# Four of the sixteen layer-1 tiles by seven half products in four more blocks, fixed staging tiles, and a later check of the softmax sums

## The chip, the cores and the metric

The kernel runs on one core of a Trainium2 chip. The core has TensorE for matrix products (PE in the profile; PEld are its weight loads), VectorE (DVE), ScalarE (ACT), GpSimd (POOL) and SyncE (SP, which here only issues DMAs). Each has its own instruction queue and works through it in order; they meet at semaphores. Matrix products end in PSUM, which has eight banks of 128 x 512 float32. The metric is the time of one execution in microseconds on the device: the median of the runs shown. Beside it stands one execution under the profiler, from which all the rows come.

## The reference

```python
k_all = np.concatenate([beacon_k, k], axis=2)          # 16 + 576 keys
scores = scale * q @ k_all^T, causal on the 576
a = softmax(scores);  x = a @ v_all                    # 8 batches, 8 heads, 64 wide
...
x = x.transpose(0, 2, 1, 3).reshape(8, 576, 512)
h = x.transpose(0, 2, 1) @ U @ V                       # rank 32, over the sequence
u = x + h.transpose(0, 2, 1)
out = u + np.maximum(u @ w_ch1, 0.0) @ w_ch2           # 512 -> 2048 -> 512
```

So: causal attention with 16 extra keys, a low-rank mix over the sequence, and a two-layer network with a residual. Inputs and output are float32; the kernel multiplies in float16 and sums in float32.

## The kernel before, in words

**Two streams on one TensorE.** Attention goes by pairs of heads, p = 0 to 31, four pairs to a batch: scores (L409), exponentials on ACT (L418), the causal mask as a minimum on DVE (`masks_of`, L348), the product with v (L427), and the division by the sum on DVE (L435, L436). The last holds the reciprocals of all softmax sums in `rec`. The network goes by blocks of 512 tokens out of 8 x 576 = 4608, so there are nine blocks, 0 to 8. `mix` and `mix_units` make u of a finished batch and put it, transposed, into the ring `uT` of 2304 columns; block 4 starts at column 2048, so its 512 tokens wrap round (`u_cols` gives two pieces of 256).

**The order is written by hand.** `feed` turns each block whose u is there into a list of units and appends them to `queue`. `fill(n)` takes n units from it; each unit taken also issues one entry of `coming` (loads and other POOL work) and counts down stores. `long_slot` (L1383) lays, for batches 3 to 7, scores, masks, outputs and `fill` calls of one pair in a row: about 30 units to a batch, as many as a block has. So the units of a block lie between the attention of the next batches. What is emitted first comes first in each engine's queue.

**A block.** Layer 1 makes `gT`, sixteen tiles of 128 x 512 of the hidden layer. In blocks 1 to 6 `g_unit` (L628) makes one a unit: four matmuls over the four chunks of the 512 inputs into one bank, then a relu out of it, on DVE in units 2, 5, 11 and 13, on ACT in the others. Layer 2 uses a 2 x 2 scheme with seven products in place of eight: tokens and outputs are halved, `sums` (L617) forms four combinations of `gT` on DVE (from unit 8 on, by the table `SUMS`), `halves_of_w2` once those of the weights, and `c_unit` (L833) issues seven products of two units, 16 matmuls of 256 columns each, into banks named A to F; `after` adds them up on DVE, POOL adds u (`residual`), SP stores.

**Blocks 7 and 8** come after the last attention. There `g_quads` (L649) makes twelve of the sixteen layer-1 tiles by the same scheme with seven products: three sets q = 0, 1, 2 of four tiles, with halves of the inputs and of the tokens. Bank A takes a product, ACT copies it, the next product is added on it in the bank, and so on (`copied`, `half`); bank D does likewise; `summed` adds a copy to F or D on DVE and `relu` follows. `quad_weights` (L580) makes the combined weights on POOL, four sums a set, 12 in all, started at pair 29. Four differences of u (L655) are made by DVE within the block. Their tiles come from the rotating pool `stage` (two buffers to each of two tags), which holds the loaded q and k of the batches before; `kept` is a pool of three float32 tiles. Layer 2 of these blocks is `chain_units`.

**PSUM by a list.** `pst` gives out the eight banks in the order in which they were last emptied, as emitted. A bank that is held over several units is missing from the round.

**The check.** `guard` (L997) compares all sums in `rec` with bounds, nine small instructions on DVE. `guard_sum` adds up over the partitions with one matmul and copies the verdict to `badi`. Every engine then loads it (L1462), and at the end branches into a slower general path if it is not zero. `guard` is emitted after the last attention, `guard_sum` six units before the end of block 7, the load twelve units before the end of block 8.

Of the kernel before, what the change touches and what calls it, by code (L numbers as in the profile page):

```python
# [9 lines left out]
F16 = mybir.dt.float16  # L10
BF16 = mybir.dt.bfloat16
F32 = mybir.dt.float32
# [18 lines left out]
def kernel(  # L31
# [220 lines left out]

    def qk_tiles():

        t = [stage.tile([P, TJ * DM], F16, name=f"st{i}", tag=f"st{i}") for i in range(2)]
# [192 lines left out]
    def mix_units(xb, u0, turned=True):  # L448
# [47 lines left out]
        def end():  # L496
            n = nq[NT - 1]
            ups = pst([P, NCC, n], F32, name="uend")
            for cc in range(NCC) if not turned else ():
                x_into(xb, ups[:, cc, :], cc, [NT - 1], QM, cc == 0)  # L500
            for cc in range(NCC):
                nc.tensor.matmul(
                    ups[:, cc, :], cell["q"], Vend[:, cc, :], start=turned and cc == 0, stop=True,
                    skip_group_check=True,
                )
            settle(1, uT[:, :, ds(u0 % RING + QM, n)], ups)
            emptying(ups)

# [57 lines left out]

    lq = {}

    def quad_tiles():

        t = [stage.tile([P, TJ * DM], F16, name=f"lw{i}", tag=f"st{i}") for i in range(2)]
        w = [[x[:, ds(512 * k, 512)] for k in range(4)] for x in t]
        w.append([pairs.tile([P, 512], F16, name=f"lw{k}", tag=f"pr{k % 2}") for k in range(4)])
        lq["w"] = [[x.rearrange("p (c f) -> p c f", c=2) for x in y] for y in w]
        lq["t"] = [x[:, ds(4 * 512 + 512 * k, 512)].rearrange("p (c x) -> p c x", c=2) for x in t for k in range(2)]
        f = [stage.tile([P, 3, 512], F32, name=f"lk{i}", tag=f"st{i}") for i in range(2)]
        k = [x[:, i, :].rearrange("p (i x) -> p i x", i=2) for x in f for i in range(3)]
        lq["k"] = [(k[2 * q], k[2 * q + 1], k[2 * q]) for q in range(3)]

    def quad_weights(q):  # L580

        def part(c0, d):
            return w1[:, ds(c0, 2), ds(P * d, 2 * P)]

        a11, a12, a21, a22 = part(0, 2 * q), part(2, 2 * q), part(0, HF + 2 * q), part(2, HF + 2 * q)
        s1, s2, s3, s4 = lq["w"][q]
        return [
            lambda o=o, x=x, y=y, op=op: nc.gpsimd.tensor_tensor(out=o, in0=x, in1=y, op=op)
            for o, x, y, op in (
                (s1, a21, a22, ALU.add), (s2, s1, a11, ALU.subtract),  # L590
                (s3, a11, a21, ALU.subtract), (s4, a12, s2, ALU.subtract),
            )
        ]

    def fast_units(t0, dst, last=False, quads=False):


        cell, banks, obs = {}, {}, {}
        cols = u_cols(t0, 512)

# [27 lines left out]
        def g_unit(k):  # L628
            if k == 0:
                begin()  # L630
            dc = order[k]
            g = pst([P, 512], F32, name="gps")
            for cc in range(NCC):
                for at, o, w in cols:
# [3 lines left out]
                    )  # L638
            if k % 2 and cell["turns"]:
                cell["turns"].pop(0)()  # L640
            for x in SUMS.get(k, ()):
                sums(*x)
            if k in (2, 5, 11, 13):
                nc.vector.tensor_scalar_max(out=cell["g"][:, dc, :], in0=g, scalar1=0.0)  # L644
# [4 lines left out]
        def g_quads():  # L649

            at = t0 % RING
            b11, b12, b21, b22 = (uT[:, ds(c, 2), ds(at + x, HT)] for c in (0, 2) for x in (0, HT))
            t1, t2, t3, t4 = lq["t"]
            us = [
                lambda o=o, x=x, y=y: nc.vector.tensor_tensor(out=o, in0=x, in1=y, op=ALU.subtract)  # L655
                for o, x, y in ((t1, b12, b11), (t2, b22, t1), (t3, b22, b12), (t4, b21, t2))
            ]
            held = {}

            def plain(dc):  # L660
                g = pst([P, 512], F32, name="gps")
                for cc in range(NCC):
                    nc.tensor.matmul(  # L663
                        g, w1[:, cc, ts(dc, P)], uT[:, cc, ds(at, 512)], start=cc == 0, stop=cc == NCC - 1
                    )
                nc.scalar.activation(out=cell["g"][:, dc, :], in_=g, func=AF.Relu)
                emptying(g)

# [13 lines left out]
            def of_lw(q, k):  # L682
                return lambda c, i: lq["w"][q][k][:, c, ts(i, P)]

            def copied(q, k):
                nc.scalar.activation(out=lq["k"][q][k], in_=held[q, "A"], func=AF.Copy)  # L686

            def summed(q, bank, k, d, x):
                nc.vector.tensor_tensor(
                    out=cell["g"][:, ds(d, 2), ds(x, HT)], in0=held[q, bank], in1=lq["k"][q][k], op=ALU.add  # L690
                )
# [4 lines left out]
            def step(q, n):  # L696
# [16 lines left out]
                else:  # L713
# [6 lines left out]
                    relu(cell["g"][:, :, HT:512].rearrange("p (h d) t -> p h d t", h=2)[:, :, ds(d, 2), :])  # L720

            slots = [
                (0, 0), (1, 0), (2, 0), (0, 1), (1, 1), (2, 1), (0, 2, 1, 2), (2, 2), 6, 14,
# [5 lines left out]
            def unit(k, slot):  # L729
# [4 lines left out]
                if isinstance(slot, int):  # L734
                    plain(slot)
                else:
# [94 lines left out]
        ]  # L831

        def c_unit(k, j):  # L833
            bank = products[k][0]
            p = pieces(bank)[j]
            product(*products[k], *p)
            for x in sums_at.get(2 * k + j, ()):
                sums(*x)
            if j == 1:
                after(k)  # L840

        def chain_units():

            halves = [(0, 0, HC), (1, 0, HC)]
            small = [(0, 0, HC), (1, 0, P), (1, P, P)] if last else halves

            def grown(k, name, i, c0, w):
                _, a, bm, _ = products[k]
                fresh = (name, i, c0) not in banks
                if fresh:  # L850
                    banks[name, i, c0] = pst([P, w], F32, name="mps" + name)
                ps = banks[name, i, c0]
                for d in range(HF):
                    nc.tensor.matmul(  # L854
                        ps, a()[:, d, ds(P * i, P)], bm[:, d, ds(c0, w)],
                        start=fresh and d == 0, stop=d == HF - 1, skip_group_check=True,
                    )
                return ps

            def first(i, c0, w):  # L860
                ps = grown(0, "A", i, c0, w)
                if i == 0:
                    kept("s1")
                nc.scalar.activation(out=cell["s1"][:, i, :], in_=ps, func=AF.Copy)

# [50 lines left out]
        if quads:  # L916
            return g_quads() + chain_units()
        units = [lambda k=k: g_unit(k) for k in range(NDC)]
        units += [lambda k=k, j=j: c_unit(k, j) for k in range(7) for j in range(len(pieces(products[k][0])))]
# [102 lines left out]
    def load_batch(b):  # L1022
        if b < DT0:
            Ls[b] = qk_tiles()
            emit_loads(b, Ls[b], vss[b % 2])
# [4 lines left out]
    def load_whole(b):  # L1030

        Ls[b] = qk_tiles()
        for i, (src, m) in enumerate(((k[b], nk), (q[b], nq))):
# [128 lines left out]
    FAST = 1  # L1162
    QUADS = (7, 8)
    SUMS = {
# [15 lines left out]
    def fill(n):  # L1180
        while n > 0 and queue:
# [9 lines left out]
            n -= 1  # L1191

    def feed(b):

        while state["t"] < NBLK and 512 * (state["t"] + 1) <= S * (b + 1):
# [7 lines left out]
            else:  # L1203
                units = fast_units(512 * t, dst, t == NBLK - 1, t in QUADS)
            queue.extend(units)
# [41 lines left out]
    with tc.manual_schedule(engines={ENG.PE, ENG.Activation, ENG.DVE, ENG.SP, ENG.Pool}):  # L1247
# [24 lines left out]
        emit_w1(0)  # L1272
        Ls[1] = qk_tiles()
        (kt, qt), _ = Ls[1]
# [187 lines left out]
        n_bad = nc.values_load(badi[0:1, 0:1], min_val=0, max_val=P)  # L1462
# [102 lines left out]
```

## Time and profile before

| | |
|---|---|
| median of 3 runs | 336.14 us (336.02 to 337.72) |
| the profiled execution | 336.39 us, its span 334.5 us |
| clock granted to TensorE | 1.00 |
| PE busy | 326.3 us, 98% of the span |
| DVE, ACT, POOL busy | 251.7, 190.8, 148.5 us |
| blocks 3, 4, 5, 6 start (layer 1) | 146.0, 180.6, 215.3, 249.9 us |
| blocks 7 and 8 start | 279.3, 304.4 us |
| last matmul ends about | 329.4 us |

Times in the profile count from the start of the span. A row of a group gives the line of the kernel, the engine, the operation with output and input tiles, the count, then the busy time, the mean of one in ns, and how long the engine stood idle ahead of them and for what. A row of a timeline gives start, length, engine, line and count; in square brackets is the idle time before it and who ended it. Matmul durations include the way through the array; the distance of starts tells the rate. The same holds in part for DVE, where the next instruction can start a little before the row of the last one ends.

### The profile page before, as it was taken

To read this page: it belongs to the slowest core of one execution; us is meant where nothing else is said; L and a number is where in the kernel's file an instruction comes from. 1 tells how busy PE (TensorE), PEld (TensorE's weight loads), DVE (VectorE), ACT (ScalarE), POOL (GpSimd) and SP (SyncE) were. 2 spreads that over 40 slices of the span, in tenths; PEclk is the share of its full clock that TensorE was granted. 3 is DMA by queue.
4 is the path that set the end of the run, shared out by engine and by line. 5 is a ranking of instruction groups with operands and counts; after the bars stand their busy time and mean duration, and the time that the engine had idled before them with its cause. 6 is when DMAs were issued, how large, how long until landed. Compare 5 with 4: busy or idle time off the path is not lost.

```text
span 334.5 us, 9085 instructions
## 1 busy us (share of the span) xinstructions
PE 326.3 (98%) x3614; PEld 223.9 (67%) x3614; DVE 251.7 (75%) x572; ACT 190.8 (57%) x413; POOL 148.5 (44%) x185
## 2 busy tenths in 40 slices
PE   8899999999999999999999999999999999999993
PEld 3565555555577656865588888754875588788793
DVE  6675888678897668765777677667777978797692
ACT  5967961788972677257734684469435403703700
POOL 8987824766236540677066904150398014010010
PEclk9999999999999999999999999999999999999999
DMA  8999999999999993999999996955213513206113
GB/s 164 144 176 161 158 201 196 199 184 151 81 150 150 135 181 74 130 200 171 151 124 174 144 132 110 117 130 120 51 42 94 91 47 110 49 32 127 31 36 101
DMA packets 150561, 41.99 MB, mean 126 GB/s; under 512 B 131312, under 2 KB 149936, under 8 KB 150512
## 3 DMA queue, kind: packets, MB, share of 16 engines
q0 software_dynamic: 87568, 18.18, 73.3%
q1 hardware_dynamic: 62144, 22.41, 36.5%
q10 hardware_dynamic: 800, 0.75, 0.7%
q8 instruction: 30, 0.49, 0.6%
q14 instruction: 19, 0.16, 0.2%
HBM read 37.45 MB, written 9.44 MB: 140 GB/s over the span
## 4 chain that ended last, share of the span: by engine, by line
PE 91%; ACT 5%; DVE 1%; issue 0%
PE gps L635 24%; PE po L427 8%; PE mpsD L760 6%; PE sps L409 6%; PE mpsF L760 4%; PE cps L965 4%; PE mpsA L854 4%; PE gps L939 4%; PE mpsE L760 3%; PE qpsA L674 3%; PE mpsC L760 3%; PE mpsA L760 3%; PE mpsB L760 3%; ACT expt L376 2%; PE mpsD L854 2%; PE gps L663 2%
## 5 line engine op out<-in xcount | busy, mean ns | idle before, releaser
L418 ACT ACTIVATE expt<-sps 128x496 f16<-128x496 f32 (+2 forms) x192 | 82.2, 547 | 41.6 <-PE sps L409 41.6
L635 PE MATMUL gps<-uT,w 128*128 128x512 f16 (+1 forms) x448 | 91.9, 349 | 0.2 <-ACT kT L1091 0.2
L780 POOL TENSOR_TENSOR ob<-ob,ut 128x512 f32<-128x512 f32 x26 | 31.3, 1207 | 131.2 <-DVE ob L780 121.5
L760 PEld LDWEIGHTS <-gT 128*128 128x128 f16 x704 | 66.4, 98 | 10.4 <-issue 2.6
L635 PEld LDWEIGHTS <-w 128*128 128x128 f16 x448 | 40.4, 98 | 32.0 <-issue 2.5
L646 ACT ACTIVATE gT<-gps 128x512 f16<-128x512 f32 x72 | 42.9, 619 | 25.2 <-PE gps L635 19.9
L624 DVE TENSOR_TENSOR gT<-gT 128x1024 f16<-128x1024 f16 (+3 forms) x90 | 47.5, 550 | 1.0
L240 POOL DMA_DIRECT2D vs<-in_v_dram x50 | 39.9, 812 | 14.1 <-DMA w<-in_moe_w_ch_dram 11.1
L427 PEld LDWEIGHTS <-expt 128*128 128x128 f16 x900 | 33.8, 98 | 9.8 <-issue 1.5
L427 PE MATMUL po<-vs,expt 128*128 128x65 f16 x900 | 36.4, 194 | 0.3
L348 DVE TENSOR_TENSOR expt<-expt,bigmask 128x768 f16<-128x768 f16 x54 | 34.4, 676 | 1.4 <-ACT expt L418 1.2
L436 DVE TENSOR_TENSOR xb<-po,rec 128x320 f16<-128x320 f32 x64 | 31.5, 492 | 2.2
L435 DVE RECIPROCAL rec<-po 128x5 f32<-128x5 f32 x64 | 12.1, 189 | 19.5 <-PE po L427 19.1
L644 DVE TENSOR_SCALAR gT<-gps 128x512 f16<-128x512 f32 x24 | 16.6, 690 | 13.1 <-PE gps L635 12.6
L686 ACT ACTIVATE lk<-qpsA 128x512 f32<-128x512 f32 x18 | 10.3, 597 | 25.6 <-PE qpsA L674 14.8
L409 PE MATMUL sps<-qT,kT 64*128 64x80 f16 (+4 forms) x288 | 22.6, 281 | 0.0
L376 ACT ACTIVATE expt<-sps 128x496 f16<-128x496 f32 (+2 forms) x48 | 20.4, 569 | 0.7 <-PE sps L370 0.7
L854 PEld LDWEIGHTS <-gT 128*128 128x128 f16 x208 | 19.0, 98 | 2.4
L1038 POOL DMA_DIRECT2D st<-in_q_dram x20 | 16.9, 866 | 6.9 <-DVE ob L780 6.5
L409 PEld LDWEIGHTS <-kT 64*128 64x128 f16 x288 | 10.3, 94 | 12.8 <-issue 8.2
L1038 POOL DMA_DIRECT2D st<-in_k_dram x20 | 16.9, 859 | 1.5 <-DMA st<-in_q_dram 1.5
L939 PE MATMUL gps<-uT,w 128*128 128x512 f16 x64 | 16.2, 380 | 0.1
(151 smaller groups left out, 479.3 us busy)
## 6 DMA issues: line engine op xcount, KB each, us to landing
out_dram<-ob SPq DMA_DIRECT2D x33, 256.0 KB, 3.6
vs<-in_v_dram POOLq DMA_DIRECT2D x18, 128.0 KB, 6.9
w<-in_moe_w_ch_dram POOLq DMA_DIRECT2D x4, 512.0 KB, 6.4
w<-in_moe_w_ch_dram POOLq DMA_DIRECT2D x2, 1024.0 KB, 12.8
st<-in_k_dram POOLq DMA_DIRECT2D x12, 128.0 KB, 6.3
st<-in_q_dram POOLq DMA_DIRECT2D x12, 128.0 KB, 7.0
st<-in_k_dram POOLq DMA_DIRECT2D x4, 288.0 KB, 11.8
st<-in_q_dram POOLq DMA_DIRECT2D x4, 288.0 KB, 12.9
```

What stands on the lines that cost most here:

```text
L240: nc.gpsimd.dma_start(out=dst[a : a + nq[j], j, :, :], in_=src[hs, ds(q0[j], nq[j]), :].rearrange("h p d -> p h d"))
L348: nc.vector.tensor_tensor(out=e, in0=e, in1=bigmask[:, :, :].rearrange("p (a b) x -> p a b x", b=2), op=ALU.min)
L409: nc.tensor.matmul(banks[i][:, ds(at0 + o, w)], kT(hp, c, ch), qT[hp, c, ds(qa, w)], start=True, stop=True, skip_group_check=len(unit) > 1,)
L418: nc.scalar.activation(out=at[p][3][i][:, ds(AT[g], gw[g])], in_=bank[:, ds(at0, gw[g])], func=AF.Exp, scale=scale)
L427: nc.tensor.matmul(po[:, j, :], ex[0 : nk[c], ds(blk[(c, j)], P)], vs[0 : nk[c], ds(c * H * E + h * E, E)], start=(c == 0), stop=(c == j),)
L436: nc.vector.tensor_tensor(out=xb[:, :, ds(h * D, D)], in0=po[:, :, 0:D], in1=r.broadcast_to([P, NT, D]), op=ALU.mult)
L624: nc.vector.tensor_tensor(out=o[:, ds(d0, n)], in0=x[:, ds(d0, n)], in1=y[:, ds(d0, n)], op=op)
L635: nc.tensor.matmul(g[:, ds(o, w)], w1[:, cc, ts(dc, P)], uT[:, cc, ds(at, w)], start=(cc == 0 and o == 0), stop=(cc == NCC - 1), skip_grou ...
L646: nc.scalar.activation(out=cell["g"][:, dc, :], in_=g, func=AF.Relu)
L760: nc.tensor.matmul(ps, a()[:, d, ds(P * i, P)], bm[:, d, ds(c0, w)], start=fresh and d == 0 and i == 0, stop=d == HF - 1, skip_group_check ...
L854: nc.tensor.matmul(ps, a()[:, d, ds(P * i, P)], bm[:, d, ds(c0, w)], start=fresh and d == 0, stop=d == HF - 1, skip_group_check=True,)
L1038: coming.append(lambda d=dst, s=src, a=m[j] - nq[j], n=m[j], j=j: nc.gpsimd.dma_start(out=d[a:n, j, :, :], in_=s[:, ds(q0[j], nq[j]), :].r ...
```

## The change

Blocks 3 to 6 get `PARTS` 1: in layer 1 set 0 (tiles 0, 1, 8, 9) is made by `g_quads`' seven half products, in four units of 8, 8, 4 and 8 matmuls of 256 columns; the other twelve tiles stay plain, three of their relus on DVE. The number of units, 16 and 14, is as before. The sums of `gT` start in unit 11 instead of 8. The differences of u for the next block (`u_sums`) are made on DVE in units 10 to 13 of the layer 2 before. In layer 2 of these blocks the second product is added onto the first one's bank, after ACT has copied that, and ACT copies the result out; before, it had a bank of its own and a DVE addition. Blocks 7 and 8 have the three sets as before; set 0's copies lie in `kept` tiles and its weights in the `pairs` tiles, made from pair 15 on.

The pool `stage` gives way to four tiles that are allotted once; batch b loads into tiles 2 (b mod 2) and the next one, and the differences of u have the last sixth of each, which the whole-batch loads of batches 4 to 7 leave free.

`guard` moves from the end of the attention to after unit 4 of block 8, `guard_sum` to after the second unit of block 8's layer 2, the load of the verdict from twelve to eight units before the end.

```diff
-    stage = ctx.enter_context(tc.tile_pool(name="stage", bufs=2))
...
+    staged = [const.tile([P, TJ * DM], F16, name=f"st{i}", tag=f"st{i}") for i in range(4)]
...
+        t = staged[2 * (b % 2) : 2 * (b % 2) + 2]
...
+    def quad_tiles(q):
+
+        if q == 0:
+            w = [pairs.tile([P, 512], F16, name=f"lw{k}", tag=f"pr{k % 2}") for k in range(4)]
+        else:
+            w = [staged[q - 1][:, ds(512 * k, 512)] for k in range(4)]
+            f = staged[q + 1][:, 0 : 2048].bitcast(F32).rearrange("p (k i x) -> p k i x", k=2, i=2)
+            lq["k", q] = (f[:, 0], f[:, 1], f[:, 0])
+        lq["w", q] = [x.rearrange("p (c f) -> p c f", c=2) for x in w]
...
+    def u_sums(t0, eng):
+
+        b11, b12, b21, b22 = (u_half(t0, c, x) for c in (0, 2) for x in (0, HT))
+        t1, t2, t3, t4 = (staged[i][:, 5 * DM : 6 * DM].rearrange("p (c x) -> p c x", c=2) for i in range(4))
...
+        return [lambda a=a: one(*a) for a in ((t1, b12, b11), (t2, b22, t1), (t3, b22, b12), (t4, b21, t2))]
...
+            def plain(k, dc):
+                layer_one(dc, not quads and k in (2, 11, 13))
...
+            def space(q, k):
+                if k < 2:
+                    cell["k", q, k] = lq["k", q][k] if q else kept("k")
+                else:
+                    cell["k", q, k] = cell["k", q, 0]
+                return cell["k", q, k]
...
+            if not quads:
+                slots = [2, (0, 0), 10, (0, 1), 3, 11, (0, 2), 4, (0, 3), 12, 5, 13, 6, 14, 7, 15]
+                late = {11: ((0, 0, 4),), 12: ((1, 0, 4),), 13: ((2, 0, 4),), 14: ((0, 4, 3),), 15: ((1, 4, 3),)}
...
+        if parts:
+            sums_at = {0: ((2, 4, 3),), 1: ((0, 7, 1), (1, 7, 1)), 2: ((2, 7, 1), (3, 0, 4)), 3: ((3, 4, 4),)}
...
+        def first(i, c0, w):
+            ps = grown(0, "A", i, c0, w)
+            if i == 0:
+                kept("s1")
+            nc.scalar.activation(out=cell["s1"][:, i, :], in_=ps, func=AF.Copy)
+
+        def second_on(i, c0, w):
+
+            ps = grown(1, "A", i, c0, w)
+            if i == 0:
+                out_tile("11")
+            nc.scalar.activation(out=obs["11"][:, i, :], in_=ps, func=AF.Copy)
+            freed(("A", i, c0))
+            if i:
+                residual("11", 0, 0)
...
-    QUADS = (7, 8)
+    PARTS = {3: 1, 4: 1, 5: 1, 6: 1, 7: 3, 8: 3}
+    AHEAD = 10
...
+            if p == P6 + 3:
+                quad_tiles(0)
+                coming.extend(quad_weights(0))
             if p == NP - 3:
-                quad_tiles()
-                coming.extend([u for q in range(3) for u in quad_weights(q)])
+                for n in (1, 2):
+                    quad_tiles(n)
+                    coming.extend(quad_weights(n))
...
-        guard()
-
-
-        queue.insert(len(queue) - 37, guard_sum)
-        fill(len(queue) - 12)
+        queue.insert(len(queue) - 26, guard)
+
+        queue.insert(len(queue) - 14, guard_sum)
+        fill(len(queue) - 8)
```

More of the change, by code (lines that the diff above doesn't have):

```diff
@@ L630, in g_unit, with between, layer_one @@
                 begin()
-            dc = order[k]
+            def between():
+                if k % 2 and cell["turns"]:
+                    cell["turns"].pop(0)()
+                for x in SUMS.get(k, ()):
+                    sums(*x)
+            layer_one(order[k], k in (2, 5, 11, 13), between)
+        def layer_one(dc, on_vector, between=lambda: None):
             g = pst([P, 512], F32, name="gps")
@@ L638, in g_unit @@
                     )
[L639 to L643, printed above, removed]
+            between()
+            if on_vector:
                 nc.vector.tensor_scalar_max(out=cell["g"][:, dc, :], in0=g, scalar1=0.0)
@@ L720, in step, with unit @@
                     relu(cell["g"][:, :, HT:512].rearrange("p (h d) t -> p h d t", h=2)[:, :, ds(d, 2), :])
+            if not quads:
+                slots = [2, (0, 0), 10, (0, 1), 3, 11, (0, 2), 4, (0, 3), 12, 5, 13, 6, 14, 7, 15]
+                late = {11: ((0, 0, 4),), 12: ((1, 0, 4),), 13: ((2, 0, 4),), 14: ((0, 4, 3),), 15: ((1, 4, 3),)}
+                def unit(k, slot):
+                    if k == 0:
+                        begin()
+                    plain(k, slot) if isinstance(slot, int) else step(*slot)
+                    if k % 2 and cell["turns"]:
+                        cell["turns"].pop(0)()
+                    for x in late.get(k, ()):
+                        sums(*x)
+                return [lambda k=k, slot=slot: unit(k, slot) for k, slot in enumerate(slots)]
             slots = [
@@ L845, in chain_units @@
             small = [(0, 0, HC), (1, 0, P), (1, P, P)] if last else halves
[L847 to L864, printed above, removed]
             def second(i, c0, w):
```

93 lines of the change are left out of this document (52 added, 41 removed).

## The prediction

> **What bounds the kernel now.** I read the page first, then the waits of TensorE (PE), the table of windows cut at block borders, the chain that ended last, the groups by shape, and the timelines of single blocks.
>
> ```profile
> span 334.5 us, 9085 instructions
> PE 326.3 (98%) x3614; PEld 223.9 (67%) x3614; DVE 251.7 (75%) x572; ACT 190.8 (57%) x413; POOL 148.5 (44%) x185
> ```
> ```profile
> PE gps L635 <- ACT kT L1091: 0.2, 1, 0.2
> ```
> ```profile
> 146.00:165.24 19.24, 19.24 (x206) 10.27 (x205) 13.14 (x27) 14.28 (x30) 11.09 (x14) 1.00 2.12 180
> 165.24:180.58 15.34, 15.34 (x170) 12.56 (x169) 11.64 (x25) 6.47 (x16) 7.35 (x8) 1.00 1.31 139
> ...
> 304.40:317.06 12.66, 12.66 (x103) 9.81 (x101) 9.69 (x21) 8.63 (x15) 0.00 (x0) 1.00 0.45 76
> 317.06:334.50 17.44, 12.27 (x128) 11.02 (x126) 11.28 (x25) 1.36 (x3) 1.16 (x1) 0.99 0.21 66
> ```
>
> The window columns are length, then busy time (and instructions) of PE, its weight loads, DVE, ACT and POOL, then PE's granted clock. The first two windows are layer 1 and layer 2 of block 3, the last two block 8 with the tail. PE is busy for all of each but the last, at full clock, and from block 1 on its list of waits has the one row of 0.2 us. A busy PE could still hide a slow rate, so I took the rate from the chain (start, length, pieces):
>
> ```profile
> 150.03 4.42 PE gps L635 x20
> ...
> 163.04 1.73 PE gps L635 x8
> ...
> 197.76 1.75 PE gps L635 x16
> ...
> 284.63 1.31 PE qpsA L674 x12
> ```
>
> A 512-column matmul takes 1.73/8 = 0.216 us, a 256-column one 1.31/12 = 0.109 us, in block 7's half products too: time goes by columns. What takes columns away here shortens the run, if nothing new makes PE wait.
>
> **The change: TensorE.** In blocks 3 to 6 four of the sixteen layer-1 tiles (16 matmuls of 512 columns, 16 x 0.216 = 3.46 us) become seven half products of four matmuls of 256 (28 x 0.109 = 3.06 us): 0.40 us less. Block 4 wraps round the ring, so its plain tiles already are 32 matmuls of 256 columns (32 x 1.75/16 = 3.50 us): 0.44 less. Sum: 3 x 0.40 + 0.44 = **1.65 us** (unrounded). Layer 2 keeps its seven products; that the second lands on the first one's bank changes no column. Blocks 7 and 8 keep their matmuls.
>
> The Trainium skill, "TensorE: Matmul & The Clock Gate", section Back-to-back issue gap, speaks against this: it gives about 131 ns sustained for 512 columns and 81 ns for 128. My estimate between them for 256 is 98 ns, so 28 x 98 = 2.74 us against 16 x 131 = 2.10 us, 0.65 us slower a block, 336.1 + 4 x 0.65 = 338.7 in all. The rows above do not show that; the section's isolated gap (518 and 262 cycles) agrees with them.
>
> **Work beside it.**
>
> ```profile
> L646 ACT ACTIVATE gT<-gps 128x512 f16<-128x512 f32 x72 | 42.9, 619 | 25.2 <-PE gps L635 19.9 <-issue 4.3 <-ACT ob L980 0.7
> L624 DVE TENSOR_TENSOR gT<-gT 128x1024 f16<-128x1024 f16 x38 | 27.0, 727 | 0.0
> L644 DVE TENSOR_SCALAR gT<-gps 128x512 f16<-128x512 f32 x24 | 16.6, 690 | 13.1 <-PE gps L635 12.6
> L686 ACT ACTIVATE lk<-qpsA 128x512 f32<-128x512 f32 x18 | 10.3, 597 | 25.6 <-PE qpsA L674 14.8 <-DVE ob L780 10.7
> L689 DVE TENSOR_TENSOR gT<-qpsD,lk 128x512 f16<-128x512 f32 x12 | 7.9, 685 | 4.1 <-ACT lk L686 2.2 <-PE qpsD L674 1.9
> L674 PEld LDWEIGHTS <-lw 128*128 128x128 f16 x96 | 9.3, 98 | 1.3 <-issue 0.2
> L588 POOL TENSOR_TENSOR lw<-w 128x512 f16<-128x512 f16 x6 | 7.2, 1208 | 0.0
> L780 DVE TENSOR_TENSOR ob<-mpsF,kept 128x512 f32<-128x512 f32 x8 | 5.5, 691 | 4.4 <-PE mpsF L760 4.4
> L797 ACT ACTIVATE kept<-mpsA 128x512 f32<-128x512 f32 x6 | 3.6, 597 | 8.6 <-PE mpsA L760 8.6
> L694 DVE TENSOR_SCALAR gT<-gT 128x1024 f16<-128x1024 f16 x6 | 2.6, 427 | 0.2
> L694 DVE TENSOR_SCALAR gT<-gT 128x512 f16<-128x512 f16 x6 | 1.8, 294 | 0.2
> L864 ACT ACTIVATE kept<-mpsA 128x256 f32<-128x256 f32 x4 | 1.5, 384 | 1.5 <-PE mpsA L854 1.5
> ```
> ```profile
> L655 DVE TENSOR_TENSOR lw<-uT,lw x4: 418/422/1261, 280.4 to 308.7; 128x512 f16<-128x512 f16 x4
> ```
>
> DVE in layer 1 gets three sums out of PSUM (3 x 0.685), two relus (0.427 + 0.294), loses one relu (0.690) and passes one of the gT sums (0.727) on to layer 2: +1.36, so 14.5 of 18.8 us. In layer 2 it gets that sum and four sums of u for the next block (4 x 0.42) and loses the add of product F (0.691): +1.72, so 13.4 of 15.3. ACT swaps three relus (0.619) for three copies and a relu (4 x 0.597, the relu at the copies' price), +0.53; in layer 2 four half copies (0.384) replace one (0.597), +0.94. Neither engine fills its window, so these cost nothing unless one comes late. The four POOL sums of weights for set 0 are not new: they move forward from the run-up to block 7 to batch 3's last head pair. That is 4 x 1.21 = 4.8 us of POOL's queue, one sum to a unit; a load queued after them slips by those 4.8 us at most. First use is in unit 3 of block 3, over twenty units later, so I put it at nothing; without that cover it would be 4.8 us, once.
>
> A sum of u took 0.42 us, but once 1.26, when a POOL add ran beside it. The Trainium skill, "GPSIMD Engine Reference", section Specifications, says GpSimd shares SBUF interfaces with VectorE when an instruction reads two SBUF inputs; the trace agrees, 1.26 against 0.42. So a sum of u costs 0.42 to 1.26; I take 0.42, the median.
>
> **Hand-offs that can make PE wait.** Block 3, start of layer 1:
>
> ```profile
> 144.36 0.69 DVE L780 TENSOR_TENSOR ob<-mpsE,kept 128x512 f32<-128x512 f32 x1 [1.86 <-PE mpsE L760]
> 144.97 1.98 DVE L348 TENSOR_TENSOR expt<-expt,bigmask 128x768 f16<-128x768 f16 x2
> ...
> 148.68 0.19 DVE L435 RECIPROCAL rec<-po 128x5 f32<-128x5 f32 x1 [0.50 <-PE po L427]
> 148.91 0.49 DVE L436 TENSOR_TENSOR xb<-po,rec 128x320 f16<-128x320 f32 x1
> ```
> ```profile
> 149.86 2.01 ACT L418 ACTIVATE expt<-sps 128x496 f16<-128x496 f32 x4 [1.05 <-PE sps L409]
> 151.73 1.12 ACT L646 ACTIVATE gT<-gps 128x512 f16<-128x512 f32 x2
> ```
>
> Of the four sums of u two fall into DVE's 1.86 us of idle time before 144.36, two behind the masks, so DVE falls 0.8 us behind. Step 0 of the set then puts a sum and a relu (0.98 us) ahead of the second division of an attention output, where 0.5 us of idle time takes part of it: that division ends at about 150.7 instead of 149.4. It frees a bank. With A and D held, two banks fewer go round, and I count the next user of this one as layer 1's unit 4, at 150.03 + 0.88 = 150.9: 0.2 us of cover. ACT: the copy of step 1 starts at 151.73, behind four exponentials, and ends at 152.33; A's next half starts at 150.03 + 3 x 0.884 = 152.7. Its copy, behind two relus, ends at about 154.0, and step 3 starts at about 154.4 (today's five tiles end at 154.45; less 0.44, and one attention output between); the sum from D ends 0.7 later, 0.2 before D's second half. So the margins are 0.2 to 0.4 us, in each of four blocks. I take 0: below nothing is excluded, since PE waits for none of these now; above, a missed hand-off costs its lateness, at most the 0.41 of a block in the rival below.
>
> Layer 2, where product B needs the last of its gT sums:
>
> ```profile
> 159.67 0.69 DVE L644 TENSOR_SCALAR gT<-gps 128x512 f16<-128x512 f32 x1 [1.46 <-PE gps L635]
> 160.28 1.02 DVE L348 TENSOR_TENSOR expt<-expt,bigmask 128x768 f16<-128x768 f16 x2
> ...
> 165.91 1.28 DVE L624 TENSOR_TENSOR gT<-gT 128x768 f16<-128x768 f16 x4
> ```
> ```profile
> 169.56 0.55 PE mpsB L760 x5
> ```
>
> Today those sums end at 165.91 + 1.28 = 167.2 and B starts at 169.6. In the new order they begin with unit 11, whose relu starts at about 159.3 (0.41 earlier). Laid end to end from there: two relus 1.4, masks 1.0, three large sums 2.2, two at most as large 1.5, two divisions 1.4, and the four pieces of the last row 1.3, in all 8.8, so 168.1 at the latest. B then starts at 169.2: at least 1 us of cover.
>
> **The check of the sums and the fixed tiles.**
>
> ```profile
> 261.30 0.33 DVE L999 MEMSET good<- 128x320 f16 x1
> ...
> 263.87 0.16 DVE L1007 TENSOR_SCALAR bad<-allg 128x1 f16<-128x1 f32 x1
> ```
> ```profile
> 308.73 0.42 DVE L655 TENSOR_TENSOR lw<-uT,lw 128x512 f16<-128x512 f16 x1
> 310.78 1.89 DVE L689 TENSOR_TENSOR gT<-qpsD,lk 128x512 f16<-128x512 f32 x3 [1.63 <-ACT lk L686]
> 313.62 0.69 DVE L689 TENSOR_TENSOR gT<-qpsD,lk 128x512 f16<-128x512 f32 x1 [0.96 <-PE qpsD L674]
> ```
> ```profile
> L1462 PEldq TENSOR_LOAD <-badi x1: 487/487/487, 318.4 to 318.4; - x1
> ```
>
> The check is 2.7 us of DVE (261.3 to 264.0), in layer 1 of block 6, where it also was late work. It now follows unit 4 of block 8, right behind 308.73. There DVE idles 1.63 and then 0.96 us, so the three sums from D slip by about 1.1 us and the next by 0.2. PE needs the first of the three at 313.0 and gets it at about 312.6. The load of the verdict moves by four units, behind a sum that is done by then. Cost 0; without that idle time up to 1.1 us, once; a gain of one load (0.49) is possible. The fixed tiles hold the same batches in the same memory; only what a load waits for can change, and PE's waits show no load after the start: 0.
>
> **Sum.** 1.65 us against the profiled execution: 336.39 (span 334.5 and 1.9 around it) to 334.74, on the median 336.14 - 1.65 = **334.5**, 0.49% faster. About 0.5% (334.46) is what a measurement can tell from no change, so the forecast sits on that line.
>
> **Rivals.** *Given back at hand-offs*: for it, margins of 0.2 to 0.4 us; against, each holds on paper. With 0.41 us of waits in each block nothing is left: 336.1. *More than the columns*: the verdict's load drops from the tail, 334.5 - 0.5 = 334.0; against it, PE loses nothing visible there now. *Slower, sums late for product B*: all four sums of u at 1.26 (+3.4 us of DVE) and no idle time to recover in; decides from 1 us of lag at unit 11, then B waits 2.4 us in each block: 334.5 + 4 x 2.4 = 344.1. Against it, the 4.3 us that DVE idles in layer 1. *Slower, small matmuls pay for their weights*: the load's 98 ns comes on top of the 109 ns, 28 x 0.207 = 5.8 against 3.46 us, +2.3 in four blocks: 345.5. The row of 12 in 1.31 us stands against that. The Trainium skill's sustained figures, above, are a milder case of it. *The change does not do what it says*, PE follows the exponentials of ACT and the columns become idle time: 336.1 again, counted with the first; ACT's 14.28 of 19.24 us speaks against.
>
> **Chances.** Forecast 0.70, half of it beyond 0.5%; more 0.03; given back 0.20; sums late 0.05; weights 0.02. Faster 0.35 + 0.03 = 0.38, same 0.35 + 0.20 = 0.55, slower 0.07. Range: 333.9 (with the gain of a load) to 336.2 (all given back).
>
> **What would show it.** Right: layer 1 of blocks 3, 5, 6 shorter by 0.4 us, PE busy throughout, no wait at the new lines, layer 2 as before. Wrong: gaps of PE at the second or third half on A, a plain tile late behind the fourth division, a gap ahead of B, a stall in block 8 behind the check, or half products above 0.44 us per four.

## The result, and the profile after

| | before | after |
|---|---|---|
| median, nine runs each | 335.6 us (335.31 to 337.72) | 334.03 us (333.70 to 334.53) |
| ratio after / before | | 0.9944 [0.9927, 0.9962] |
| the profiled execution, its span | 336.39, 334.5 us | 334.53, 332.9 us |
| body: first plain tile of block 3 to the end of the last product | 183.50 us | 182.28 us |

The changed kernel is faster, by 1.57 us between the medians. The ratio goes by the means (335.97 and 334.10 us), in which before's longest run of 337.72 weighs more. The forecast was 1.65 us and 334.5 us. The page of after:

```profile
span 332.9 us, 9194 instructions
PE 324.4 (97%) x3646; PEld 226.9 (68%) x3646; DVE 264.9 (80%) x600; ACT 195.8 (59%) x429; POOL 149.3 (45%) x185
```

PE is busy 1.9 us less, with 32 matmuls more, and DVE 13 us more. The list of PE's waits has, from block 1 on, a row that before's has not:

```profile
PE sps L410 <- DVE ob L820: 0.2, 1, 0.2
```

The windows of after, with the columns as in the prediction (layer 1 and layer 2 of block 3):

```profile
146.51:165.35 18.84, 18.84 (x218) 11.42 (x217) 14.36 (x32) 14.70 (x31) 11.08 (x14) 1.00 2.10 148
165.35:180.69 15.34, 15.34 (x170) 12.54 (x169) 13.38 (x28) 7.23 (x19) 7.46 (x8) 1.00 1.35 142
```

Layer 1 of block 3 is 18.84 us long against 19.24, layer 2 is 15.34 as before, and PE is busy throughout. DVE has 14.36 us in layer 1 (14.5 forecast) and 13.38 in layer 2 (13.4 forecast).

The start of block 3 lies up to 1.7 us apart in the profiles of the kernels here (145.5 to 147.2), so I compare lengths. The body begins with the first plain tile of block 3, in PE's timeline, and ends with the last product, in the chain that ended last. Before, in these two views:

```profile
145.84 1.03 PE L635 MATMUL gps<-uT,w 128*128 128x512 f16 x4
```
```profile
327.56 1.78 PE mpsD L854 x24
```

After:

```profile
146.34 1.03 PE L664 MATMUL gps<-uT,w 128*128 128x512 f16 x4
```
```profile
326.84 1.78 PE mpsD L880 x24
```

Before: 327.56 + 1.78 - 145.84 = 183.50. After: 326.84 + 1.78 - 146.34 = 182.28, so 1.22 less. By blocks, from first tile to first tile, blocks 3, 4 and 5 took 34.58, 34.74 and 34.58 us before and 34.19, 34.30 and 34.18 after: 0.39, 0.44 and 0.40 less, the forecast's columns within a hundredth. Block 6 has as many columns fewer and did not get shorter. PE there, before (first plain tile, third scores of the batch, the tile behind them, first half product of block 7):

```profile
249.74 1.03 PE L635 MATMUL gps<-uT,w 128*128 128x512 f16 x4
...
253.34 0.39 PE L409 MATMUL sps<-qT,kT 64*128 64x336 f16 x6
253.66 2.55 PE L635 MATMUL gps<-uT,w 128*128 128x512 f16 x11
...
279.11 0.60 PE L674 MATMUL qpsA<-uT,w 128*128 128x256 f16 x4
```

and after:

```profile
249.01 1.03 PE L664 MATMUL gps<-uT,w 128*128 128x512 f16 x4
...
252.62 0.31 PE L410 MATMUL sps<-qT,kT 64*128 64x336 f16 x1
253.10 0.37 PE L410 MATMUL sps<-qT,kT 64*128 64x336 f16 x5 [0.17 <-DVE ob L820]
253.41 0.61 PE L690 MATMUL qpsA<-st,lw 128*128 128x256 f16 x4
...
278.46 0.60 PE L690 MATMUL qpsA<-uT,w 128*128 128x256 f16 x4
```

The block took 279.11 - 249.74 = 29.37 us before and 278.46 - 249.01 = 29.45 after. The scores take 253.41 - 252.62 = 0.79 us from start to next start instead of 0.32. The list of waits says 0.2 us, since one matmul of the group had run and its modelled end covers part of the gap; the distance of starts gives the whole of it, 0.47 us. That is block 6's 0.40 of columns and a little more. The releaser is DVE's last addition of the layer 2 before, which empties the bank that these scores go to. DVE in after, up to that addition:

```profile
245.62 1.03 DVE L593 TENSOR_TENSOR st<-uT 128x512 f16<-128x512 f16 x1
246.69 1.26 DVE L593 TENSOR_TENSOR st<-uT,st 128x512 f16<-128x512 f16 x1
247.87 0.68 DVE L820 TENSOR_TENSOR ob<-mpsE,kept 128x512 f32<-128x512 f32 x1
248.47 2.34 DVE L349 TENSOR_TENSOR expt<-expt,bigmask 128x768 f16<-128x768 f16 x2
250.73 1.38 DVE L593 TENSOR_TENSOR st<-uT 128x512 f16<-128x512 f16 x1
252.04 0.41 DVE L593 TENSOR_TENSOR st<-uT,st 128x512 f16<-128x512 f16 x1
252.37 0.68 DVE L820 TENSOR_TENSOR ob<-mpsD,kept 128x512 f32<-128x512 f32 x1
```

and POOL beside it, making the weight sums of sets 1 and 2:

```profile
246.33 1.34 POOL L605 TENSOR_TENSOR st<-w 128x512 f16<-128x512 f16 x1
...
248.93 1.47 POOL L605 TENSOR_TENSOR st<-w,st 128x512 f16<-128x512 f16 x1
250.36 1.47 POOL L820 TENSOR_TENSOR ob<-ob,ut 128x512 f32<-128x512 f32 x1
```

Three of the four sums of u take 1.03, 1.26 and 1.38 us, the fourth, with POOL idle from 251.83, takes 0.41. The addition ends at 252.37 + 0.68 = 253.05, and PE goes on at 253.10.

### The profile page after: what moved, and what is told of

It is laid out like the page before. It is cut to its first block, busy times and chain, and to the rows that moved or that the text cites. A ratio compares the mean times of both kernels' runs of the same rounds, so it can differ in the third digit from the quotient of the medians.

```text
span 332.9 us, 9194 instructions
## 1 busy us (share of the span) xinstructions
PE 324.4 (97%) x3646; PEld 226.9 (68%) x3646; DVE 264.9 (80%) x600; ACT 195.8 (59%) x429; POOL 149.3 (45%) x185
## 4 chain that ended last, share of the span: by engine, by line
PE 86%; DVE 6%; ACT 5%; DMA 1%; issue 1%; DVEq 0%
PE gps L664 21%; PE mpsA L880 8%; PE po L428 8%; PE sps L410 6%; PE mpsD L800 5%; PE qpsA L690 5%; PE cps L1019 4%; PE gps L993 4%; PE mpsB L800 3%; PE mpsE L800 3%; PE mpsC L800 3%; PE qpsD L690 3%; PE mpsF L800 2%; PE mpsD L880 2%; ACT expt L377 2%; ACT w L377 2%
## 5 line engine op out<-in xcount | busy, mean ns | idle before, releaser
L664 PE MATMUL gps<-uT,w 128*128 128x512 f16 (+1 forms) x400 | 84.9, 354 | 0.2 <-ACT kT L1145 0.2
L664 PEld LDWEIGHTS <-w 128*128 128x128 f16 x400 | 36.6, 98 | 29.0 <-issue 1.8
L672 ACT ACTIVATE gT<-gps 128x512 f16<-128x512 f32 x68 | 40.6, 618 | 19.6 <-PE gps L664 14.1
L709 ACT ACTIVATE kept<-qpsA 128x512 f32<-128x512 f32 x18 | 10.8, 602 | 22.6 <-PE qpsA L690 12.0
L670 DVE TENSOR_SCALAR gT<-gps 128x512 f16<-128x512 f32 x20 | 13.8, 689 | 11.4 <-PE gps L664 11.3
L880 PE MATMUL mpsA<-w,gT 128*128 128x256 f16 x160 | 19.0, 273 | 0.0
```

The costliest lines, as they stand in the source:

```text
L664: nc.tensor.matmul(g[:, ds(o, w)], w1[:, cc, ts(dc, P)], uT[:, cc, ds(at, w)], start=(cc == 0 and o == 0), stop=(cc == NCC - 1), skip_grou ...
L880: nc.tensor.matmul(ps, a()[:, d, ds(P * i, P)], bm[:, d, ds(c0, w)], start=fresh and d == 0, stop=d == HF - 1, skip_group_check=True,)
```

## The experiments

My theory after the result: the gain is the columns of blocks 3 to 6, and block 6 loses its share in that one wait, because DVE works through the sums of u beside POOL's weight sums. The rivals: fixed tiles, early weights or the later check bring part of the gain; the wait at 253 is not what block 6 lost; the two additions onto one bank in layer 2 matter.

**e1_no_parts** keeps all of the change but the half products of blocks 3 to 6.

```diff
-    PARTS = {3: 1, 4: 1, 5: 1, 6: 1, 7: 3, 8: 3}
+    PARTS = {7: 3, 8: 3}
```

> The changed kernel with blocks 3 to 6 made the old way (all sixteen layer-1 tiles plain, old layer 2, no sums of u ahead); the fixed tiles, the early weights of set 0 and the late check stay. Theory (the gain is TensorE's columns): the time from block 3's first matmul to the last one is 183.3 us as before (it was 182.1 in the changed kernel), and the whole is as before within 0.2 us. Rival (the gain lies in the tail, behind the late check: from the last matmul to the end of the span 4.3 us after against 5.2 before): the span still gains some 0.9 us, and the whole is 0.9 us faster than before.

Measured: 335.33 us, ratio to before 0.9995 [0.9981, 1.0009]. The body's ends, in PE's timeline and in the chain:

```profile
145.87 1.03 PE L664 MATMUL gps<-uT,w 128*128 128x512 f16 x4
```
```profile
327.59 1.78 PE mpsD L880 x24
```

183.50 us, as before. Without the half products nothing is left of the body's gain. Of the time, the interval leaves room for 0.6 us faster to 0.3 us slower than before (the medians lie 0.28 us apart).

**e2_check_moved** is the kernel before with the check alone moved.

```diff
-        guard()
-        queue.insert(len(queue) - 37, guard_sum)
-        fill(len(queue) - 12)
+        queue.insert(len(queue) - 26, guard)
+        queue.insert(len(queue) - 14, guard_sum)
+        fill(len(queue) - 8)
```

> The kernel before with nothing changed but the place of the check, of its sum and of the verdict's load. Theory: no change within 0.2 us, the tail behind the last matmul stays near 5.2 us and moves only by what it scatters by itself. Rival (the later load shortens the tail): 0.5 to 0.9 us faster than before, tail near 4.3 us. A third: block 8 pays for the check on DVE, up to 1.1 us slower, with a gap on PE behind it.

Measured: 335.84 us, 1.0007 [0.9999, 1.0016]. The time gains nothing from the later load. The profile warns of something else: its body is 183.97 us, 0.47 more than before's. 0.25 of that is in block 5, which the edit doesn't touch: PE takes 0.78 us for eight scores there instead of 0.52, at full clock, and the trace names no engine that it waits for. A block's length in a single profile can be off by that much.

**e3_no_block6** leaves block 6 as it was.

```diff
-    PARTS = {3: 1, 4: 1, 5: 1, 6: 1, 7: 3, 8: 3}
+    PARTS = {3: 1, 4: 1, 5: 1, 7: 3, 8: 3}
```

> The changed kernel with half products in blocks 3, 4 and 5 only; block 6 the old way, and so no sums of u in block 5's layer 2. Theory (block 6 gave its 0.40 us back in one wait for a bank, 0.47 us at its third scores): the same time as the changed kernel within 0.1 us, block 3's first to the last matmul about 182.1 us, and no wait of PE at 253. Rival (each block brings 0.4 us and the wait was chance): 0.4 us slower than the changed kernel, 182.5 us.

Measured: 334.17 us, 0.9958 [0.9944, 0.9971], body 182.31 against after's 182.28 (block 5 has 0.11 more than after's here, and block 6, with 29.38, 0.07 less). PE in block 6:

```profile
252.06 0.39 PE L410 MATMUL sps<-qT,kT 64*128 64x336 f16 x6
252.38 3.84 PE L664 MATMUL gps<-uT,w 128*128 128x512 f16 x17
```

The third scores take 0.32 us again, with 0.40 us more of columns behind them. So block 6's half products gain 0.40 and lose it.

**e4_weights_early** starts the weight sums of sets 1 and 2 two head pairs earlier.

```diff
-            if p == NP - 3:
+            if p == NP - 5:
                 for n in (1, 2):
```

> The changed kernel with the POOL sums of the weights of sets 1 and 2 started two head pairs earlier, so that they are done before DVE makes the sums of u for block 6. Theory (those sums of u took 1.03, 1.26 and 1.38 us instead of 0.41 since POOL's sums ran beside them, and that made DVE late with the bank): sums of u at 0.41 to 0.5 us, no wait of PE at 253, block 3's first to the last matmul 181.7 us, 0.4 us less than the changed kernel. Rival (DVE is late from its own amount of work): the wait stays, 182.1 us. Against both: the POOL sums now stretch masks and sums of gT in block 5's layer 1 and PE waits there.

Measured: 336.41 us, 1.0017 [1.0006, 1.0028]. The wait at block 6 went: the sums of u took 0.41, 1.26, 0.41 and 0.41 us there, and the block 28.98 us, 0.39 less than before. But POOL's sums now lay in layer 1 of block 5, beside the masks and the sums of `gT`, and block 5 took 36.67 us instead of 34.18. PE's waits and one row of DVE:

```profile
PE sps L410 <- DVE xb L437: 1.2, 1, 1.2
...
PE gps L664 <- DVE xb L437: 0.5, 1, 0.5
```
```profile
229.36 2.94 DVE L349 TENSOR_TENSOR expt<-expt,bigmask 128x768 f16<-128x768 f16 x2
```

Two masks take 2.94 us where they took 1.02. The same POOL work two pairs earlier costs more than block 6 had lost. So POOL beside DVE, and not DVE's own amount of work, made the wait.

**e5_weights_split** makes set 1's weights where after does and set 2's two pairs later.

```diff
-            if p == NP - 3:
-                for n in (1, 2):
-                    quad_tiles(n)
-                    coming.extend(quad_weights(n))
+            if p in (NP - 3, NP - 1):
+                n = 1 if p == NP - 3 else 2
+                quad_tiles(n)
+                coming.extend(quad_weights(n))
```

> The changed kernel with the POOL sums of set 2's weights made two head pairs later (beside block 6's layer 1), those of set 1 where they were, so that POOL is free while DVE makes the sums of u for block 6. Theory (POOL's sums beside them made DVE late with the bank that PE's third scores of block 6 need): those sums take 0.41 us but for one beside a residual addition, no wait of PE in block 6, block 3's first to the last matmul 181.7 us against 182.1, the whole 0.4 us faster than the changed kernel. Rival (contention only moves: the later POOL sums stretch DVE work in block 6's layer 1 as they did in block 5's when they came earlier): 182.1 us or more, with a wait of PE between 255 and 268.

Measured: 334.44 us, 0.9967 [0.9955, 0.9978], body 182.62. PE's waits, and DVE in block 6:

```profile
PE qpsD L690 <- DVE gT L712: 0.7, 1, 0.7
```
```profile
251.84 1.23 DVE L717 TENSOR_SCALAR gT<-gT 128x512 f16<-128x512 f16 x1
...
254.22 2.89 DVE L349 TENSOR_TENSOR expt<-expt,bigmask 128x768 f16<-128x768 f16 x2
```

The third scores took 0.32 us again, with sums of u of 0.41, 1.26, 0.41 and 0.41. The wait had moved: POOL's sums of set 2 ran from 251.78 to 256.7, the relu of 0.29 us took 1.23, the masks 2.89, and the sum from D came 0.7 us late for D's second half.

**e6_sums_twice** makes each sum of u of blocks 3 to 6 twice over.

```diff
-            return us[n - AHEAD : n - AHEAD + 1] if n >= AHEAD else []
+            return us[n - AHEAD : n - AHEAD + 1] * 2 if n >= AHEAD else []
```

> The changed kernel with every sum of u for blocks 3 to 6 made twice in a row: DVE gets 1.7 us more ahead of each of these blocks, up to 2.5 where POOL runs beside it. Theory (in blocks 3 to 5 DVE's last addition of layer 2 frees its bank 1.5 us ahead of the scores that need it, in block 6 not at all): 0 to 1 us of waits in each of blocks 3 to 5, 1 to 2.5 more in block 6, in all 1.5 to 5 us slower than the changed kernel. Rival (the 0.2 to 0.4 us of cover that the prediction counted at the second division's bank): at least 1 us in every block, 4 us and more in all.

Measured: 338.82 us, 1.0093 [1.0077, 1.011], body 187.10, 4.8 more than after. The largest wait, in block 6:

```profile
253.58 0.62 PE L428 MATMUL po<-vs,expt 128*128 128x65 f16 x15 [1.62 <-DVE expt L349]
```

Blocks 3 and 4 took 1.35 and 1.31 us more than after's (PE waited at the third scores and at a plain tile), block 5 took no more, and block 6 took 2.17 more. The total fits the theory and the rival alike. By blocks neither holds: the theory allowed blocks 3 and 4 at most 1 us each, and the rival asked at least 1 us of block 5. The eight sums there took 0.42 to 0.44 us each and two masks 1.02, with POOL's last instruction ended at 212.6; in blocks 3 and 4, with POOL additions beside them, two of the eight took 1.71 us together and the masks 1.98. So DVE has cover for eight sums where POOL rests, and not where it adds.

**e7_old_layer2** takes layer 2 of blocks 3 to 6 from the kernel before.

```diff
-            if parts and k < 2:
-                (first, second_on)[k](*p)
-            else:
-                product(*products[k], *p)
+            product(*products[k], *p)
...
-            if j == 1 and not (parts and k < 2):
+            if j == 1:
```

> The changed kernel with layer 2 of blocks 3 to 6 as before: product F in a bank of its own, added to the first by DVE. Theory (layer 2 brings no time, it only spares DVE an addition of 0.69 us and a bank): the same as the changed kernel within 0.2 us, 182.1 us from block 3's first to the last matmul, or slightly more in block 6. Rival (the accumulation is needed, since DVE is the late engine in layer 2): 0.3 to 0.7 us more in each of four blocks, 1.2 to 2.8 us slower.

Measured: 334.08 us, 0.9951 [0.9937, 0.9964]: by time the same as after. The trace shows more. Its body is 181.88 us, 0.40 less than after's, and all of that is block 6 (29.06 us). The third scores there, and the first sum of u:

```profile
253.52 0.46 PE L410 MATMUL sps<-qT,kT 64*128 64x336 f16 x6
253.92 0.61 PE L690 MATMUL qpsA<-st,lw 128*128 128x256 f16 x4
```
```profile
246.49 0.68 DVE L593 TENSOR_TENSOR st<-uT 128x512 f16<-128x512 f16 x1
```

The scores take 0.40 us, so 0.08 of the wait is left. In after POOL's queue is released by ACT's copy of the second product, 9.5 us before block 6; here by DVE's addition, 9.9 us before it:

```profile
239.53 1.15 POOL L820 TENSOR_TENSOR ob<-ob,ut 128x512 f32<-128x512 f32 x1 [15.23 <-ACT ob L897]
```
```profile
240.03 1.16 POOL L820 TENSOR_TENSOR ob<-ob,ut 128x512 f32<-128x512 f32 x1 [15.33 <-DVE ob L820]
```

So the weight sums run 0.4 us earlier, and the first sum of u takes 0.68 instead of 1.03 us. The addition on one bank saves DVE an addition, and by this one trace it costs block 6, through POOL, what it lost.

**e8_steps_together** puts the four steps of set 0 next to each other instead of between plain tiles.

```diff
-slots = [2, (0, 0), 10, (0, 1), 3, 11, (0, 2), 4, (0, 3), 12, 5, 13, 6, 14, 7, 15]
+slots = [2, 10, 3, (0, 0), (0, 1), (0, 2), (0, 3), 11, 4, 12, 5, 13, 6, 14, 7, 15]
```

> The changed kernel with the four steps of set 0 one right behind the other (units 3 to 6) instead of with plain tiles between them. Theory (the plain tiles hide the copies that PE must wait for before it adds on bank A): between steps PE waits for ACT, 0.2 us ahead of step 1's end, 0.25 before step 2, 0.65 before step 3, and more behind the four exponentials: 1 to 2.5 us a block, 4 to 10 us slower than the changed kernel and slower than before. Rival (the copies are quick enough by themselves): within 0.5 us of the changed kernel.

Measured: 346.40 us, 1.0322 [1.0296, 1.0348], body 194.62, 12.3 more than after. PE in block 3:

```profile
152.14 0.60 PE L690 MATMUL qpsA<-st,lw 128*128 128x256 f16 x4 [1.40 <-ACT kept L709]
...
153.42 0.60 PE L690 MATMUL qpsA<-st,lw 128*128 128x256 f16 x4 [0.25 <-ACT kept L709]
154.71 0.60 PE L690 MATMUL qpsA<-st,w 128*128 128x256 f16 x4 [0.69 <-ACT kept L709]
```

Each half on bank A waits for ACT's copy of the one before it, and the first copy for the exponentials ahead of it. The theory named the wait and put it too low, at 4 to 10 us. The plain tiles between the steps are the cover.

**e10_check_old_place** is after with the check at its old place, the edit of e2 reversed.

> The changed kernel with the check, its sum and the verdict's load where they were before: right behind the last attention, in block 6's layer 1. Theory (block 6 now has little time to spare on DVE: sums of gT begin at unit 11, and 2.7 us of check come ahead of them): product B or C of block 6 waits for its sums, 0.5 to 2 us slower than the changed kernel. Rival (the place does not matter, as it did not in the kernel before, where moving it changed nothing beyond 0.2 us): within 0.2 us of the changed kernel, 182.1 us from block 3's first to the last matmul.

Measured: 334.19 us, 0.9953 [0.9937, 0.9969], body 182.27, block 6 29.45 us with the same wait. What I expected here fell: the check costs nothing in block 6 either.

**e11_again** is after, unchanged.

> The changed kernel as it is, once more beside the others. Theory (TensorE's columns less the wait in block 6): 1.2 us less than before from block 3's first to the last matmul, with the same wait of 0.5 us at block 6's third scores; the whole 1.2 to 1.6 us faster than before. Rival (the wait is chance): 1.65 us less and no such wait. The first result's 1.6 to 1.9 us would, if it comes again, ask for another 0.3 us outside this stretch.

Measured: 334.05 us, 0.9947 [0.9929, 0.9965], body 182.27, and the wait at the same scores with the same 0.17 us in its bracket. The wait belongs to the kernel.

**e12_block6_later** moves the sums of u of block 6 out of POOL's way, into its own units 4 and 5, and its steps of set 0 behind them.

```diff
+                if t0 == 512 * 6:
+                    slots = [2, 10, 3, 11, 4, 12, (0, 0), 5, (0, 1), 13, (0, 2), 6, (0, 3), 14, 7, 15]
+                    early = {4: us[0:2], 5: us[2:4]}
...
-        if PARTS.get(t, 0) != 1:
+        if PARTS.get(t, 0) != 1 or t == 6:
```

(The table of the `gT` sums follows the new order.)

> The changed kernel with block 6's set 0 made later, in units 6 to 12, and its sums of u in units 4 and 5 of block 6 itself instead of in block 5's layer 2, where POOL's weight sums stretch them; its gT sums go in smaller pieces, in the order in which their tiles are ready. Theory (DVE is late at block 6's third scores from those sums of u alone): that wait of 0.47 us is gone and the block keeps its 0.40 us: 181.7 us from block 3's first to the last matmul, 0.4 us faster than the changed kernel. Rival (the wait comes back elsewhere, ahead of product B, whose sums now end later, or at bank D): 182.1 us or more.

Measured: 334.02 us, 0.9951 [0.9934, 0.9967], body 182.13, block 6 29.30. The third scores take 0.32 us. But a new gap of 0.29 us stands ahead of D's second half, which begins 0.73 us after A's instead of 0.44. It waits for the sum from D, here in DVE's timeline:

```profile
260.69 0.69 DVE L712 TENSOR_TENSOR gT<-qpsD,kept 128x512 f16<-128x512 f32 x1 [0.47 <-ACT kept L709]
```

**e13_block6_spaced** is e12 with one plain tile more between the third and the fourth step of block 6's set 0.

```diff
-... 13, (0, 2), 6, (0, 3), 14, 7, 15]
+... 13, (0, 2), 6, 14, (0, 3), 7, 15]
```

> The kernel with block 6's set 0 made later and its sums of u in block 6 itself, and now with one more plain tile between step 2 and step 3 of that set. Theory (in the kernel without that tile PE waited 0.29 us in step 3, since the sum from bank D had not ended): no wait in step 3, block 6 takes 29.0 us from its first matmul to block 7's instead of 29.3 (29.45 in the changed kernel, 29.37 before the change), 181.8 us from block 3's first to the last matmul; the whole 1.65 us faster than the kernel before, 0.4 faster than the changed one, less than a measurement tells apart. Rival (the sums of gT now end too late for product B): a wait ahead of B, 182.1 us or more.

Measured: 333.88 us, 0.995 [0.9937, 0.9964]. PE in block 6, and the end of the chain:

```profile
249.41 1.03 PE L664 MATMUL gps<-uT,w 128*128 128x512 f16 x4
...
253.01 0.39 PE L410 MATMUL sps<-qT,kT 64*128 64x336 f16 x6
253.33 2.76 PE L664 MATMUL gps<-uT,w 128*128 128x512 f16 x12
...
278.39 0.60 PE L690 MATMUL qpsA<-uT,w 128*128 128x256 f16 x4
```
```profile
326.77 1.78 PE mpsD L892 x24
```

Block 6 takes 278.39 - 249.41 = 28.98 us, 0.39 less than before, with no wait left. The body, from 146.75, is 181.80 us: 1.70 less than before, where the columns of all four blocks are 1.65. This has the lowest median, but its time can't be told from after's, and it is one profile.

## Why the prediction was right or wrong

**The columns: right.** 0.40 us a block and 0.44 in block 4, measured 0.39, 0.44, 0.40, and 0.39 in block 6 once nothing waits there (e13). Taking the half products out took all of it back (e1). Two lines of after's chain have the rate:

```profile
151.53 1.73 PE gps L664 x8
...
153.26 0.44 PE qpsA L690 x4
```

0.216 us for 512 columns and 0.110 for 256, as before the change (0.109). The sustained figures of the Trainium skill, "TensorE: Matmul & The Clock Gate", section Back-to-back issue gap (131 and 81 ns), do not agree with this kernel's trace; its isolated gap does.

**Hand-offs at zero: wrong, in one block of four.** The step said "I take 0" after it had priced the banks, the copies and D in block 3. What it listed held. In after, DVE's second division and its sum from D, and ACT's copy of step 1:

```profile
150.41 0.49 DVE L437 TENSOR_TENSOR xb<-po,rec 128x320 f16<-128x320 f32 x1
...
154.41 0.69 DVE L712 TENSOR_TENSOR gT<-qpsD,kept 128x512 f16<-128x512 f32 x1 [1.97 <-ACT kept L709]
```
```profile
152.25 0.63 ACT L709 ACTIVATE kept<-qpsA 128x512 f32<-128x512 f32 x1
```

The division ends at 150.90, 0.5 us ahead of its bank's next tile (0.2 forecast); the copy at 152.88, 0.2 ahead of A's next half at 153.09 (0.4 forecast); the sum at 155.10, 0.19 ahead of D's second half at 155.29 (0.2 forecast). What failed is that block 3 stood for all four, with a sum of u at the median 0.42 us. Around the start of block 6 (249.01) POOL adds without a pause, weight sums and residuals, from 239.53 to 251.83, and three of the four sums of u took 1.03 to 1.38 us, at the upper end of the 0.42 to 1.26 that I had given and past it. The bank that came late was one not on the list: that of the last product of the layer 2 before. It cost 0.47 us, so the body gained 1.22 and not 1.65. *Given back at hand-offs* was the right kind of rival, with about the right price for one block (0.41), and I let it happen in all four or in none.

**Product B:** its sums of `gT` ended about 1.4 us ahead of it in block 3 (at least 1 us forecast), so that rival did not come near. **Weights on top of the matmul:** that rival would need 0.207 us for 256 columns, and the chain has 0.110.

**The check: right.** DVE in block 8 of after, the first instruction of the check and the first sum from D behind it:

```profile
308.24 0.33 DVE L1053 MEMSET good<- 128x320 f16 x1
...
310.88 0.68 DVE L712 TENSOR_TENSOR gT<-qpsD,kept 128x512 f16<-128x512 f32 x1
```

The check takes 2.7 us, as forecast, and the sum slipped by 1.0 us (block 8 starts 0.9 earlier, so 310.78 would be 309.9); PE did not wait. The rival *more than the columns* names the time that was measured, 334.0, but not its cause: with the check at its old place the time is the same (e10), and alone it brings nothing (e2).

**Fixed tiles and set 0's early weights at nothing: not contradicted.** e1 has both, with before's body and a time that can't be told from before's.

**The chances: the step that failed.** "The forecast sits on that line": the measured ratio, 0.9944, has 0.995 inside its interval, so the line was well placed. But I gave no change 0.55 (half of the forecast's 0.70, and all of *given back* with its 336.1 and 0.41 us lost in every block) and a gain 0.38. The runs showed a gain, 0.9944 with 1 outside the interval, and 0.47 us lost in block 6 and nothing in blocks 3 to 5. The columns were certain from rows, and a hand-off that fails in one block takes a quarter of them, so the chance of a plain gain should have been the larger. The time was taken from 336.14, the median of three runs; nine runs give 335.6, and that accounts for the 0.5 us between 334.5 and 334.03. That the medians' 1.57 us came so near to 1.65 is luck: the body gave only 1.22.

**Open:** the body gained 1.22 us and the medians 1.57 (1.72 in the round of e11). The rest lies outside the body, and single profiles can't place it. From the last product to the end of the span before took 5.2 us, all the others 4.2 to 4.5; but before's profiled execution was 0.8 us over its median, and e1 has 4.3 with a time that can't be told from before's. Between after and e1, which differ in blocks 3 to 6 alone, the medians are 1.30 us apart, close to the body's 1.22. Whether the other parts of the change bring the last 0.3 us, or scatter does, no run here settles. The 0.4 us of e7 and e13 show in their traces and not in their times.

## What to carry to other kernels

Cost a step that recurs in several blocks in each of them, with what the other engines do there: three blocks gave their columns within a hundredth, and the fourth, beside POOL's sums, nothing. When work is put on a side engine, look for every bank that its later instructions empty, those of the stage before too, and not only for those of the new code. Read a small wait by the distance of starts: the list said 0.2 us where 0.47 were lost.

## What the runs showed of the hardware

Most DVE instructions that work on SBUF alone become longer while POOL adds two tiles: a sum of u 1.03 to 1.38 us against 0.41, two masks 1.98 to 2.94 against 1.02, and a relu with one input 1.23 against 0.29, while DVE's additions out of PSUM stayed at 0.68. The Trainium skill, "GPSIMD Engine Reference", section Specifications, names contention for DVE instructions with two SBUF inputs or in a mode that uses two ports. The trace agrees, the relu included if it runs in such a mode, which no run here shows. The price is the rest of the POOL addition: in after the sums of u that start at 245.62, 246.69 and 250.73 end 0.27 to 0.28 us behind POOL additions that end at 246.38, 247.67 and 251.83, and e7's first sum 0.29 behind one. The other order occurs as well: in e4 a sum of `gT` that began 0.08 us ahead of a POOL addition kept its 0.68 us, and POOL's took 1.62 instead of 1.15. So POOL, with 149.3 us of 332.9 busy and no wait of PE put down to it, set the only wait that the change brought.
